# A two-layer attention and feed-forward kernel: values of every second key tile in column groups, V in columns of 17, K and Q weights with their columns in turns in one tile

## The chip, the cores and the metric

One core of one Trainium2 chip. The metric is the device time of one execution in microseconds, the median of a few runs. Engines named here: PE (TensorE, the matmul array), DVE (VectorE), ACT (ScalarE), POOL (GpSimd), SP (SyncE, which only issues transfers). SBUF is the working memory with 128 partitions, PSUM the memory that matmuls write to.

## The reference

`x` has 2048 rows of 512 values in bf16. The same two blocks are applied twice, with the same weights both times:

```python
def attention(x, wqkv, wo):            # 32 heads of 16 columns
    q, k, v = split(x @ wqkv)
    p = softmax(q @ k.T * 16 ** -0.5)  # 2048 x 2048 for each head
    return concat(p @ v) @ wo

x = x + attention(layernorm(x), wqkv, wo)
x = x + silu(layernorm(x) @ w1) @ w2   # w1 is 512 x 1792
x = x + attention(layernorm(x), wqkv, wo)
x = x + silu(layernorm(x) @ w1) @ w2
```

## The kernel before

**Tiles.** Rows are taken in 16 tiles of 128 (`TT`), and queries in 4 chunks `c` of 512 rows (`NQC`). The 32 heads are taken in 8 head groups `hb` of 4 (`HB`). A head has 16 columns, and each head sits in a strip of 32 partitions: in `KT` and `QT`, head `j` of a group is in partitions 32j to 32j+15, row 32j+16 holds a one (K) or a bound on the score with a minus sign (Q), and the rest is zero. So one matmul over 32 rows gives the scores minus their bound, and the exp needs no maximum. The zeros come from padded weights: `wk_pad` and `wq_pad` hold each head's 16 weight columns followed by 16 zeros. POOL clears both (L81, L82) and copies the columns in (L114, L118) from `wraw`, the transferred weights.

**The loop.** A *unit* is one key tile `kt` of one head group of one chunk: 4 x 8 x 16 = 512 units in a layer. In a unit, `emit_s` (L518) makes the scores of the *next* unit: 4 matmuls, one for each head, each on its own 32 rows, into two PSUM tiles of two banks (`wide`, 3 buffers). ACT makes two exps (L586), each of 128x1024, from PSUM into `p_sb` (5 buffers). Then `emit_pv` (L530) multiplies by the values, 4 matmuls into `o_ps` (one buffer of one bank, 128 partitions x 512): two of the second exp of the unit before and two of the first exp of this unit. In a unit with `kt` = 0 only the two of the unit before are issued, and unit 1 then has six.

**The values** for head `j` come from `vdq`: a 128x128 operand that is zero but for columns 32j to 32j+15, which hold V, and column 32j+16, which holds ones, so that row 32j+16 of `o_ps` is the sum of the exps. POOL fills these operands from V, for 4 key tiles at a time into one of two slots (`vd_fill`, L139; `NG` = 4, `NR` = 2), 4 copies each, one for each head.

**The end of a head group.** When a head group's last values are in, DVE copies `o_ps` to `oT` (L574), PE transposes it (L337), DVE divides by the sums (L343, L344). These stand first in the queue described next.

**The pump.** All other work is cut into small steps in a queue, `Pump` (L487); each unit runs `todo` of them after its value matmuls, one in most units, two where many are left. A step is mostly two matmuls of 512 columns. In chunk 0 the steps are the K projections of the next head group (`k_piece`, L234); in every chunk the Q projection of the next (`q_piece`, L294); in chunks 1 to 3 the output projection of the chunk before (L355), its feed-forward part (L411), and in layer 0 the next layer's normalisation and V (`next_pieces`, L450). The order on PE, ACT and DVE is the order in which the program writes it; POOL's is set by a scheduler.

**Start and ends.** At the start the four chunks are normalised: statistics on DVE (L150, L151), a root on ACT, `xn` on DVE (L183), transposes on PE (L195), a copy on DVE (L196). Then follow K for head group 0 (`k_two`, L250), the largest K values (`amax_bm`, L260), Q (L294) and, in layer 0, V (`v_two`, L288). Between the layers and at the end, the last chunk's projection and feed-forward part (`ffn_last`, L468) run by themselves.

Of the kernel before, what the change touches and what calls it, by code (L numbers as in the profile page):

```python
# [9 lines left out]
ALU = mybir.AluOpType  # L10
# [8 lines left out]
def kernel(  # L19
# [17 lines left out]
    H = 32  # L37
# [9 lines left out]
    VS = DH + 1  # L47
    KR = 32
    NG = 4
    NR = 2  # L50
# [6 lines left out]
    vpool = ctx.enter_context(tc.tile_pool(name="vpool", bufs=2))  # L57
    qpool = ctx.enter_context(tc.tile_pool(name="qpool", bufs=3))
# [6 lines left out]
    small = ctx.enter_context(tc.tile_pool(name="small", bufs=4))  # L65
# [13 lines left out]
    wq_pad = wpool.tile([P, CT, H, 32], BF16, name="wq_pad")  # L79
    wk_pad = wpool.tile([P, CT, H, 32], BF16, name="wk_pad")  # L80
    nc.gpsimd.memset(wk_pad[:], 0.0)  # L81
    nc.gpsimd.memset(wq_pad[:], 0.0)  # L82
    cw = cpool.tile([P, 256], BF16, name="cw")
    nc.vector.memset(cw[:], 0.0)
    nc.vector.memset(cw[0:1, 128:129], 1.0)
    for j in range(4):
        nc.vector.memset(cw[0:1, 32 * j + 16 : 32 * j + 17], 1.0)
# [6 lines left out]
    onescol = cpool.tile([P, 1], FP32, name="onescol")  # L94
    mc_ps = narrow("mc_ps")
    nc.tensor.matmul(mc_ps[:, 0:1], lhsT=cw[0:1, 0:128], rhs=cw[0:1, 128:129], start=True, stop=True)
    nc.vector.tensor_copy(out=onescol[:], in_=mc_ps[:, 0:1])


# [9 lines left out]
    w2_sb = wpool.tile([P, FT, D], BF16, name="w2_sb")  # L109
    wraw = htpool.tile([P, CT, 2 * D], BF16, name="wraw", tag="ht")  # L110
    nc.scalar.dma_start(wraw[:], A_wqkv[:, 0 : 2 * D].rearrange("(ct p) f -> p ct f", p=P))
    nc.scalar.dma_start(wv_sb[:], A_wqkv[:, 2 * D : 3 * D].rearrange("(ct p) f -> p ct f", p=P))
    for ct in range(CT):
        nc.gpsimd.tensor_copy(  # L114
            out=wk_pad[:, ct, :, 0:DH],
            in_=wraw[:, ct, D : 2 * D].rearrange("p (h d) -> p h d", d=DH),
        )
        nc.gpsimd.tensor_copy(  # L118
            out=wq_pad[:, ct, :, 0:DH],
            in_=wraw[:, ct, 0:D].rearrange("p (h d) -> p h d", d=DH),  # L120
        )
# [7 lines left out]
    vs = [vpool.tile([P, TT, D], BF16, name=f"v{i}", tag="v") for i in range(2)]  # L129
    vdq = []  # L130
    for i in range(NR):
        vd = xpool.tile([P, NG, 4, P], BF16, name=f"vd{i}")
        nc.gpsimd.memset(vd[:], 0.0)
        for j in range(4):
            nc.gpsimd.memset(vd[:, :, j, 32 * j + DH : 32 * j + DH + 1], 1.0)
        vdq.append(vd)


    def vd_fill(va, hb, g, slot):  # L139
        for j in range(4):  # L140
            h = 4 * hb + j
            nc.gpsimd.tensor_copy(  # L142
                out=vdq[slot][:, :, j, 32 * j : 32 * j + DH],
                in_=va[:, NG * g : NG * (g + 1), DH * h : DH * (h + 1)],
            )
# [78 lines left out]
    def k_mm(xnT, hb, ps, cts):  # L224
        for ct in cts:
            nc.tensor.matmul(  # L226
                ps,
                lhsT=wk_pad[:, ct, 4 * hb : 4 * hb + 4, :].rearrange("p h s -> p (h s)"),
                rhs=xnT[:, ct, :],
                start=(ct == 0),  # L230
                stop=(ct == CT - 1),
            )

    def k_piece(xnTs, c, hb):  # L234
        cell = {}

        def a():
            cell["ps"] = narrow("k_ps")
            k_mm(xnTs[c], hb, cell["ps"][:, :], (0, 1))

        def b():
            k_mm(xnTs[c], hb, cell["ps"][:, :], (2, 3))
            nc.vector.tensor_scalar(  # L243
                out=KT[:, hb, c * 512 : (c + 1) * 512], in0=cell["ps"][:, :],
                scalar1=onescol[:, 0:1], scalar2=None, op0=ALU.add,
            )

        return [a, b]

    def k_two(xnTs, c, hb):  # L250
        k_ps = wide("k2_ps")
        for i in range(2):
            k_mm(xnTs[c + i], hb, k_ps[:, i, :], range(CT))
        nc.vector.tensor_scalar(
            out=KT[:, hb, c * 512 : (c + 2) * 512],
            in0=k_ps[:].rearrange("p a b -> p (a b)"),
            scalar1=onescol[:, 0:1], scalar2=None, op0=ALU.add,
        )

    def amax_bm(hb):  # L260
        nc.vector.tensor_reduce(
            out=amax[:, hb : hb + 1], in_=KT[:, hb, :], axis=AX.X, op=ALU.max,
            apply_absolute_value=True,
        )
        nc.vector.tensor_scalar_mul(out=Bm[:, hb, :], in0=E[:, :], scalar1=amax[:, hb : hb + 1])
# [8 lines left out]

    def v_piece(cellx, tt, va):
        cell = {}

        def a():
            cell["ps"] = narrow("v_ps")
            v_mm(cellx["xnT"], tt, cell["ps"][:, :], (0, 1))  # L280

        def b():
            v_mm(cellx["xnT"], tt, cell["ps"][:, :], (2, 3))
            nc.vector.tensor_copy(out=va[:, tt, :], in_=cell["ps"][:, :])

        return [a, b]

    def v_two(xnT, tt, va):  # L288
        ps = wide("v2_ps")
        for i in range(2):  # L290
            v_mm(xnT, tt + i, ps[:, i, :], range(CT))
        nc.vector.tensor_copy(out=va[:, tt : tt + 2, :], in_=ps[:, :, :])

    def q_piece(xnTs, c, hb, QTs):  # L294
        cell = {}

        def mm(cts):
            for ct in cts:
                nc.tensor.matmul(  # L299
                    cell["ps"][:, :],  # L300
                    lhsT=wq_pad[:, ct, 4 * hb : 4 * hb + 4, :].rearrange("p h s -> p (h s)"),
                    rhs=xnTs[c][:, ct, :],
                    start=(ct == 0),
                    stop=(ct == CT - 1),
                )
# [5 lines left out]
        def b():  # L311
            mm((2, 3))
            qc = qwork.tile([P, 512], BF16, name="qc", tag="qc")
            nc.vector.tensor_copy(out=qc[:], in_=cell["ps"][:, :])  # L314
# [7 lines left out]
        def d():  # L322
            nc.tensor.matmul(  # L323
                cell["ps"][:, :], lhsT=Bm[:, hb, :], rhs=cell["qu"][:], start=False, stop=True,
                skip_group_check=True,
            )
            QTs[c][hb] = qpool.tile([P, 512], BF16, name="QT", tag="qt")
            nc.vector.tensor_copy(out=QTs[c][hb][:], in_=cell["ps"][:, :])  # L328
# [84 lines left out]
    def ffn_pieces(c, emit_out):  # L413
        cell = {}
        pieces = ln_steps(c, cell)
        for ft in range(FT):
# [11 lines left out]
            def d(ft=ft, hc=hc):  # L428
                t_sb = tpool.tile([P, 2, 512], FP32, name="t_sb", tag="t")
                nc.scalar.activation(t_sb[:, 0, :], hc["ps"][:, :], ACT.Tanh, scale=0.5)  # L430
                nc.vector.scalar_tensor_tensor(  # L431
                    out=cell["hT"][:, ft, :], in0=t_sb[:, 0, :], scalar=1.0, in1=hc["ps"][:, :],
# [35 lines left out]
    def ffn_last(c, emit_out):  # L468
# [3 lines left out]
        for f2 in range(FT // 2):  # L472
# [3 lines left out]
            t_sb = tpool.tile([P, 2, 512], FP32, name="t_sb", tag="t")  # L476
# [41 lines left out]
    def emit_s(QT, hb, kt):  # L518
        tiles = [wide("s_ps") for _ in range(2)]
        for j in range(4):  # L520
            nc.tensor.matmul(  # L521
                tiles[j // 2][:, j % 2, :],
# [5 lines left out]
        return tiles  # L528

    def emit_pv(o_ps, p_sb, kt, pr):  # L530
        for jj in range(2):
            j = 2 * pr + jj
            nc.tensor.matmul(  # L533
                o_ps[:, :],
                lhsT=vdq[kt // NG % NR][:, kt % NG, j, :],
                rhs=p_sb[:, jj, :],
                start=(kt == 0 and j == 0),
                stop=(kt == TT - 1 and j == 3),
            )

# [10 lines left out]
    for L in range(2):  # L551
# [17 lines left out]
        s_now = emit_s(QTs[0][0], 0, 0)  # L569
# [6 lines left out]

        for u, (c, hb, kt) in enumerate(units):
            if kt == 0:
                if hb == 0:
                    old_attn, attn_c = (attn, c - 1)  # L580
                    new_attn = apool.tile([P, 4, D], BF16, name="attn", tag="attn")

            ps = []
            for pr in range(2):
                p_sb = ppool.tile([P, 2, 512], BF16, name="p_sb", tag="p")
                nc.scalar.activation(  # L586
                    p_sb[:].rearrange("p a b -> p (a b)"),
                    s_now[pr][:].rearrange("p a b -> p (a b)"),
                    ACT.Exp,
                    scale=float(SCALE),  # L590
                )
                ps.append(p_sb)

            if u + 1 < len(units):
                nc_, nhb, nkt = units[u + 1]
                s_now = emit_s(QTs[nc_][nhb], nhb, nkt)

            if kt == 0:
                for args in pend:
                    emit_pv(*args)  # L600
                pend = []
# [10 lines left out]
                pend = [(o_ps, ps[0], 0, 0), (o_ps, ps[1], 0, 1)]  # L612
# [11 lines left out]
            else:  # L624
                pend.append((o_ps, ps[0], kt, 0))
                for args in pend:
                    emit_pv(*args)
                pend = [(o_ps, ps[1], kt, 1)]

            if kt % NG == 0 and u > 0 and u + NG * (NR - 1) < len(units):  # L630
                _, fhb, fkt = units[u + NG * (NR - 1)]
                vd_fill(va, fhb, fkt // NG, fkt // NG % NR)
# [5 lines left out]
            if left and kt < TT - 2 and pump.q:  # L638
                todo = max(todo, 1)
            pump_some(todo)  # L640
# [5 lines left out]
        for args in pend:  # L646
            emit_pv(*args)
# [37 lines left out]
```

## Time and profile before

| | us |
|---|---|
| median of 3 runs (2173.24 to 2178.0) | 2176.86 |
| the profiled execution's own time | 2173.48 |
| its span in the profile | 2171.7 |
| first exp of layer 0, first exp of layer 1 (start) | 64.4, 1146.6 |
| end of the last exp of layer 0, of layer 1 | 1058.0, 2111.8 |
| ACT busy, PE busy | 1942.9, 1934.3 |

Times in the profile count from the span's start. A group's line gives the source line, the engine, the operation, what it writes and reads, the count; then the busy time and the mean of one instruction in ns; then the idle time of the engine just before these instructions, and what ended it. Instructions on one engine overlap in the records, so the mean of one (1249 ns for an exp) is longer than the distance from one to the next (0.92 us). A line of waits gives the engine and what waited, for what, the sum in us, the count and the longest. A line of the windows view is a stretch of time: its length, the busy time and instruction count of each engine, then PE's granted clock (1.00 is full), the share of the DMA engines and GB/s.

### The profile page before, as it was taken

To read this page: it belongs to the slowest core of one execution; us is meant where nothing else is said; L and a number is where in the kernel's file an instruction comes from. 1 tells how busy PE (TensorE), PEld (TensorE's weight loads), DVE (VectorE), ACT (ScalarE), POOL (GpSimd) and SP (SyncE) were. 2 spreads that over 40 slices of the span, in tenths; PEclk is the share of its full clock that TensorE was granted. 3 is DMA by queue.
4 is the path that set the end of the run, shared out by engine and by line. 5 is a ranking of instruction groups with operands and counts; after the bars stand their busy time and mean duration, and the time that the engine had idled before them with its cause. 6 is when DMAs were issued, how large, how long until landed. Compare 5 with 4: busy or idle time off the path is not lost.

```text
span 2171.7 us, 28490 instructions
## 1 busy us (share of the span) xinstructions
PE 1934.3 (89%) x10355; PEld 712.9 (33%) x10561; DVE 558.7 (26%) x1106; ACT 1942.9 (89%) x2152; POOL 247.7 (11%) x1055
## 2 busy tenths in 40 slices
PE   3999988899898998999778999998999889998996
PEld 1333323333333333333232333333333333333332
DVE  6323222112311133112342322131113111131114
ACT  0899989999899998999418999999999999999981
POOL 3111111111011110111000111111111111111100
PEclk9999999999999999999789999999999999999997
DMA  4000000000000000000000000000000000000000
GB/s 145 1 1 1 1 1 1 1 1 1 1 1 1 1 1 1 1 1 1 1 0 1 1 1 1 1 1 1 3 8 1 1 1 8 4 1 1 6 5 10
DMA packets 8477, 11.79 MB, mean 5 GB/s; under 512 B 400, under 2 KB 7312, under 8 KB 8336
## 3 DMA queue, kind: packets, MB, share of 16 engines
q1 hardware_dynamic: 7280, 8.39, 1.1%
q8 instruction: 82, 1.34, 0.2%
q10 hardware_dynamic: 1056, 1.57, 0.2%
q14 instruction: 59, 0.48, 0.1%
HBM read 7.86 MB, written 2.10 MB: 5 GB/s over the span
## 4 chain that ended last, share of the span: by engine, by line
PE 62%; ACT 22%; issue 9%; DVE 6%; DMA 0%; ACTq 0%; DVEq 0%
PE o_ps L533 29%; ACT p_sb L586 20%; PE s_ps L521 16%; PE y_ps L400 3%; PE k_ps L226 3%; PE q_ps L299 2%; PE h_ps L393 2%; PE y_ps L372 2%; PE v_ps L270 2%; ACT t_sb L430 1%; DVE st L150 1%; PE t_ps L195 1%; DVE oT L574 1%; PE at_ps L337 1%; DVE hT L478 1%
## 5 line engine op out<-in xcount | busy, mean ns | idle before, releaser
L586 ACT ACTIVATE p_sb<-s_ps 128x1024 bf16<-128x1024 f32 x2048 | 1921.3, 1249 | 105.2 <-PE s_ps L521 105.2
L533 PE MATMUL o_ps<-p_sb,vd 128*128 128x512 bf16 x3909 | 1034.4, 383 | 19.6 <-issue 15.3
L521 PE MATMUL s_ps<-QT,KT 32*128 32x512 bf16 x4096 | 574.5, 383 | 89.9 <-ACT p_sb L586 85.7
L533 PEld LDWEIGHTS <-vd 128*128 128x128 bf16 x4096 | 317.7, 98 | 478.6 <-issue 237.4
L142 POOL COPY vd<-v 128x64 bf16<-128x64 bf16 x1024 | 231.1, 238 | 1850.8 <-PE o_ps L533 1708.8
L521 PEld LDWEIGHTS <-KT 32*128 32x128 bf16 x4096 | 175.2, 90 | 589.8 <-issue 569.1
L574 DVE CAST oT<-o_ps 128x512 bf16<-128x512 f32 x64 | 44.3, 692 | 381.1 <-PE o_ps L533 381.1
L431 DVE SCALAR_TENSOR_TENSOR hT<-t_sb,h_ps 128x512 bf16<-128x512 f32 x84 | 57.5, 685 | 301.7 <-ACT t_sb L430 301.7
L400 PE MATMUL y_ps<-w_sb,hT 128*128 128x512 bf16 x445 | 126.3, 383 | 5.4 <-DVE hT L478 4.5
L393 PE MATMUL h_ps<-xnT,w_sb 128*128 128x512 bf16 x438 | 127.0, 389 | 2.8 <-DVE xnT L196 1.0
L314 DVE CAST qc<-q_ps 128x512 bf16<-128x512 f32 x64 | 44.2, 691 | 170.3 <-PE q_ps L299 170.3
L243 DVE TENSOR_SCALAR KT<-k_ps,onescol 128x512 bf16<-128x512 f32 x56 | 42.0, 751 | 168.7 <-PE k_ps L226 168.7
L195 PE MATMUL t_ps<-ident,xn 128*128 128x128 bf16 x256 | 30.8, 263 | 57.2 <-DVE xn L183 55.4
L406 DVE SCALAR_TENSOR_TENSOR x_sb<-y_ps,x_sb 128x512 bf16<-128x512 f32 x32 | 22.1, 691 | 231.1 <-PE y_ps L400 231.1
L477 ACT ACTIVATE t_sb<-h_ps 128x1024 f32<-128x1024 f32 x14 | 14.3, 1023 | 74.9 <-PE h_ps L393 58.7
L430 ACT ACTIVATE t_sb<-h_ps 128x512 f32<-128x512 f32 x84 | 78.3, 932 | 0.0
L299 PE MATMUL q_ps<-xnT,wq_pad 128*128 128x512 bf16 x255 | 75.8, 380 | 2.5 <-DVE attn L344 2.4
L226 PE MATMUL k_ps<-xnT,wk_pad 128*128 128x512 bf16 x254 | 76.7, 392 | 0.3 <-issue 0.2
L393 PEld LDWEIGHTS <-w_sb 128*128 128x128 bf16 x448 | 44.8, 100 | 58.2 <-issue 8.6
L400 PEld LDWEIGHTS <-hT 128*128 128x128 bf16 x448 | 43.9, 99 | 60.1 <-DVE hT L478 5.6
L328 DVE CAST QT<-q_ps 128x512 bf16<-128x512 f32 x64 | 44.3, 692 | 36.6 <-PE q_ps L323 36.6
L372 PE MATMUL y_ps<-wo_sb,aT 128*128 128x512 bf16 x126 | 40.6, 423 | 7.6 <-DVE aT L367 7.3
(58 smaller groups left out, 568.2 us busy)
## 6 DMA issues: line engine op xcount, KB each, us to landing
w_sb<-in_B_w_dram SPq DMA_DIRECT2D x2, 1792.0 KB, 14.9
x_sb<-in_A_x_dram SPq DMA_DIRECT2D x4, 512.0 KB, 9.8
out_dram<-x_sb SPq DMA_DIRECT2D x16, 128.0 KB, 1.7
wraw<-in_A_wqkv_dram ACTq DMA_DIRECT2D x1, 1024.0 KB, 7.6
wv_sb<-in_A_wqkv_dram ACTq DMA_DIRECT2D x1, 512.0 KB, 10.0
wo_sb<-in_A_wo_dram SPq DMA_DIRECT2D x1, 512.0 KB, 12.4
```

The source lines that it names most:

```text
L142: nc.gpsimd.tensor_copy(out=vdq[slot][:, :, j, 32 * j : 32 * j + DH], in_=va[:, NG * g : NG * (g + 1), DH * h : DH * (h + 1)],)
L226: nc.tensor.matmul(ps, lhsT=wk_pad[:, ct, 4 * hb : 4 * hb + 4, :].rearrange("p h s -> p (h s)"), rhs=xnT[:, ct, :], start=(ct == 0), stop= ...
L299: nc.tensor.matmul(cell["ps"][:, :], lhsT=wq_pad[:, ct, 4 * hb : 4 * hb + 4, :].rearrange("p h s -> p (h s)"), rhs=xnTs[c][:, ct, :], star ...
L372: nc.tensor.matmul(cell["ps"][:, :], lhsT=cell["aT"][:, ct, :], rhs=wo_sb[:, ct, :], start=(ct == 0), stop=(ct == CT - 1),)
L393: nc.tensor.matmul(ps, lhsT=w1_sb[:, ct, ft * P : (ft + 1) * P], rhs=xfT[:, ct, :], start=(ct == 0), stop=(ct == CT - 1),)
L400: nc.tensor.matmul(ps, lhsT=hT[:, ft, tq * P : (tq + 1) * P], rhs=w2_sb[:, ft, :], start=(ft == 0), stop=(ft == FT - 1),)
L430: nc.scalar.activation(t_sb[:, 0, :], hc["ps"][:, :], ACT.Tanh, scale=0.5)
L431: nc.vector.scalar_tensor_tensor(out=cell["hT"][:, ft, :], in0=t_sb[:, 0, :], scalar=1.0, in1=hc["ps"][:, :], op0=ALU.add, op1=ALU.mult,)
L521: nc.tensor.matmul(tiles[j // 2][:, j % 2, :], lhsT=KT[32 * j : 32 * j + KR, hb, kt * P : (kt + 1) * P], rhs=QT[32 * j : 32 * j + KR, :], ...
L533: nc.tensor.matmul(o_ps[:, :], lhsT=vdq[kt // NG % NR][:, kt % NG, j, :], rhs=p_sb[:, jj, :], start=(kt == 0 and j == 0), stop=(kt == TT - ...
L574: nc.vector.tensor_copy(out=oT[:], in_=o_ps[:])
L586: nc.scalar.activation(p_sb[:].rearrange("p a b -> p (a b)"), s_now[pr][:].rearrange("p a b -> p (a b)"), ACT.Exp, scale=float(SCALE),)
```

## The change

- **Columns of 17.** V is kept as `va`, one for each layer: for each key tile 32 heads x 17 columns (16 of V and a one), and 15 columns more at the end. POOL sets both tiles to one at the start; V is copied into the 16 columns of each head. The two-tile V copy becomes two copies.
- **Column groups.** For odd key tiles (`COL`) the values are multiplied without `vdq`: for each head, a matmul whose stationary operand is 32 columns of `va` (the head's 17 and 15 that belong to the next) writes 32 partitions of `o_ps`. Both pairs of an odd tile are issued in the next unit. Even key tiles (`DIAG`) go as before, through `vdq`, which holds two of them a slot (`NG` = 2).
- **Weights.** `wkq` replaces `wk_pad` and `wq_pad`: 16 columns of K and 16 of Q in turns for each head. The K projection reads it from column 0 on, the Q projection from column 16. What the other operand leaves in the upper half of a strip is multiplied by zero when PSUM is copied out (`own` is one in the first 16 partitions of each strip). The Q bound is now a matmul of its own that DVE adds to `qc`.
- **Constants** (`own`, `onescol`, `one17`, `lead`) are made by DVE reductions of the identity instead of a small matmul.
- **Code that isn't used here.** `exp_passes`, `epool`'s `z`, `m` and `pd`, and `late` serve key tiles in `OFF`, which is empty: all exps stay on ACT.
- Pools: `qpool` 3 to 2 buffers, `small` 4 to 3; the second layer's `va` and the first's are separate tiles.

```diff
+    NG = 2
+    COL = [1, 3, 5, 7, 9, 11, 13, 15]
+    DIAG = [kt for kt in range(TT) if kt not in COL]
+    OFF = []
...
-    nc.gpsimd.memset(wk_pad[:], 0.0)
-    nc.gpsimd.memset(wq_pad[:], 0.0)
...
+    cols = cpool.tile([P, 4], FP32, name="cols")
+    idr = ident[:].rearrange("p (j r) -> p j r", r=32)
+    nc.vector.tensor_reduce(out=cols[:, 0:1], in_=idr[:, :, 0:DH], axis=AX.XY, op=ALU.max)
...
+    own, onescol, one17, lead = (cols[:, i : i + 1] for i in range(4))
...
+    wkq = wpool.tile([P, CT, 2 * D + DH], BF16, name="wkq")
+    nc.gpsimd.memset(wkq[:, :, 2 * D : 2 * D + DH], 0.0)
     for ct in range(CT):
+        pairs = wkq[:, ct, 0 : 2 * D].rearrange("p (h t d) -> p h t d", t=2, d=DH)
+        for t in range(2):
+            nc.gpsimd.tensor_copy(
+                out=pairs[:, :, t, :],
+                in_=wraw[:, ct, (1 - t) * D : (2 - t) * D].rearrange("p (h d) -> p h d", d=DH),
+            )
...
+    VW = VS * H + 32 - VS
+    for i in range(2):
+        va = xpool.tile([P, TT, VW], BF16, name=f"va{i}")
+        nc.gpsimd.memset(va[:], 1.0)
...
         vd = xpool.tile([P, NG, 4, P], BF16, name=f"vd{i}")
         nc.gpsimd.memset(vd[:], 0.0)
...
+                out=vdq[slot][:, :, j, 32 * j : 32 * j + VS],
+                in_=va[:, k0 : k0 + step * (NG - 1) + 1 : step, VS * h : VS * h + VS],
...
-            scalar1=onescol[:, 0:1], scalar2=None, op0=ALU.add,
+            scalar1=own, scalar2=onescol, op0=ALU.mult, op1=ALU.add,
...
-        nc.vector.tensor_copy(out=va[:, tt : tt + 2, :], in_=ps[:, :, :])
+        for i in range(2):
+            nc.vector.tensor_copy(
+                out=v_dst(va, tt + i), in_=ps[:, i, :].rearrange("p (h d) -> p h d", d=DH)
+            )
...
-            nc.vector.tensor_copy(out=qc[:], in_=cell["ps"][:, :])
+            nc.vector.tensor_scalar(
+                out=qc[:], in0=cell["ps"][:, :], scalar1=own, scalar2=one17,
+                op0=ALU.mult, op1=ALU.add,
+            )
...
-            nc.vector.tensor_copy(out=QTs[c][hb][:], in_=cell["ps"][:, :])
+            nc.vector.tensor_tensor(
+                out=QTs[c][hb][:], in0=cell["ps"][:, :], in1=cell["qc"][:], op=ALU.add
+            )
...
+    def emit_pv(o_ps, ps, hb, kt, prs, va):
+        for pr in prs:
+            for jj in range(2):
+                j = 2 * pr + jj
+                if kt in COL:
+                    h = 4 * hb + j
+                    nc.tensor.matmul(
+                        o_ps[32 * j : 32 * j + 32, :],
+                        lhsT=va[:, kt, VS * h : VS * h + 32],
+                        rhs=ps[pr][:, jj, :],
+                        start=False,
+                        stop=(kt == TT - 1),
+                        skip_group_check=True,
+                    )
+                else:
+                    d = DIAG.index(kt)
+                    nc.tensor.matmul(
+                        o_ps[:, :],
+                        lhsT=vdq[d // NG % NR][:, d % NG, j, :],
+                        rhs=ps[pr][:, jj, :],
+                        start=(kt == 0 and j == 0),
+                        stop=False,
+                        skip_group_check=True,
+                    )
...
+        def flush(u):
+            for args in pend:
+                emit_pv(*args, va)
+            pend.clear()
...
+                flush(u)
+                if off:
...
+                elif kt in COL:
+                    pend.append((o_ps, ps, hb, kt, (0, 1)))
+                else:
+                    emit_pv(o_ps, ps, hb, kt, (0,), va)
+                    pend.append((o_ps, ps, hb, kt, (1,)))
```

## The prediction

> **What bounds the kernel now.** I read the page's busy table first, then the groups, then the waits of ScalarE, then the stretches where ScalarE waits.
>
> ```profile
> span 2171.7 us, 28490 instructions
> PE 1934.3 (89%) x10355; PEld 712.9 (33%) x10561; DVE 558.7 (26%) x1106; ACT 1942.9 (89%) x2152; POOL 247.7 (11%) x1055
> L586 ACT ACTIVATE p_sb<-s_ps 128x1024 bf16<-128x1024 f32 x2048 | 1921.3, 1249 | 105.2 <-PE s_ps L521 105.2
> L533 PE MATMUL o_ps<-p_sb,vd 128*128 128x512 bf16 x3909 | 1034.4, 383 | 19.6 <-issue 15.3
> L521 PE MATMUL s_ps<-QT,KT 32*128 32x512 bf16 x4096 | 574.5, 383 | 89.9 <-ACT p_sb L586 85.7
> ...
> ACT p_sb L586 <- PE s_ps L521: 105.2, 54, 43.1
> ```
>
> PE and ACT show the same share, but the groups tell them apart. The exps fill 1921.3 us, 0.92 us each back to back, so a unit (one key tile, two exps) can't take under 1.84 us. Of the 105.2 us that exps waited for scores, 28.0 and 43.1 lie before the first exp of each layer. Only 34.1 us is left inside both attention loops: 28.4 in the first head group of chunks 1, 2 and 3 of layer 0 (9.4, 9.4 and 9.6 in the waits view), 2.0 at the start of layer 1, and the rest in pieces of 0.16 at key tile 3 of a head group. That 34.1, with some 0.1 per restart, is all that a faster PE can give back. The rest of the span is 64.4 us of start, 88.6 between the layers and 60 of tail.
>
> The second thing to see is the clock of PE and what goes before its changes (windows view: PE, PEld, DVE, ACT and POOL busy, then granted clock):
>
> ```profile
> 327.89:331.31 3.42, 1.36 (x6) 0.40 (x5) 2.93 (x16) 2.74 (x3) 0.00 (x0) 1.00 0.00 0
> 331.31:334.72 3.41, 2.97 (x15) 1.41 (x16) 1.12 (x4) 1.94 (x2) 0.43 (x2) 0.50 0.02 5
> 805.76:809.17 3.41, 2.08 (x12) 0.53 (x10) 1.01 (x3) 3.41 (x4) 0.90 (x4) 1.00 0.02 7
> 809.17:812.59 3.42, 2.64 (x9) 0.82 (x11) 0.36 (x1) 1.52 (x3) 0.00 (x0) 0.50 0.00 0
> 833.06:836.48 3.42, 2.07 (x10) 0.49 (x8) 3.01 (x14) 3.42 (x4) 0.00 (x0) 1.00 0.02 5
> 836.48:839.89 3.41, 2.48 (x22) 1.23 (x23) 2.36 (x9) 1.80 (x3) 0.45 (x2) 1.00 0.00 0
> ```
>
> The clock changes only on a grid of 3.41 us. I recounted the matmul records on that grid: a 512-column matmul is 0.213 us of array (their spacing is 0.216), a 128-column transpose a quarter of that, and a score matmul, which uses 32 of 128 rows, also a quarter. The stretches at full clock that were followed by half clock held at most 0.36 (0.27 at 327.9, 0.33 at 805.8, 0.36 at 2154.0); the emptiest that kept it held 0.375, 0.377 and 0.379 (560.0, 833.1, 1782.0). Counting scores as whole breaks the order (0.45 at 805.8 lost the clock, 0.39 at 2113.1 kept it); three eighths each also separates them (0.36 and 0.39). Of stretches at half clock, nine of 0.80 or more went back up; one of 0.81 and all of 0.63 and below stayed. The one at 805.8 is the passage between two head groups: PE waits for oT and for attn, and all it has is 4 scores, 3 value matmuls and 4 transposes.
>
> **The change part by part.**
>
> *Values.* Per pair of units PE now issues 8 full value matmuls (1.73 us). After: 4 full (0.86) and one group of four on 32 columns each. No row shows such a group. Bounds: 0.21 if four run at once, 0.87 plus a switch if they follow each other. The nearest row is the four score matmuls on 32 rows, 0.43 us from first start to the next value matmul, switch included; I take that, a saving of 0.44 us a pair. ScalarE's pace covers it in most units. It shows in two places:
> - The wait at key tile 3: there are 22 of about 0.16 idle and 0.1 restart, and unit 1 loses two of six value matmuls (0.43). All go: -5.9 (bounds 0 and -8).
> - The three first head groups of layer 0, where the pump runs two steps a unit. The waits behind them are mostly PE waiting for DVE (oT 0.79, attn 0.81, qu 1.11, aT 0.52), and these stay. Odd units lose 0.43 and even ones almost nothing: over units 1 to 12 some 2.5 each of the 10.4 (9.4 and ten restarts), -7.5 (bounds 0 and -15). Late next is the same DVE chain.
>
> *The clock.* What PE loses in matmuls it loses in occupancy. Around a head group's end (units 15 and 0, one grid stretch) there are six value matmuls now; after, two full ones and a group of four that I count as quarters: three fewer by array, 3 x 0.213 / 3.41 = 0.19 less. Such stretches stand at 0.38 to 0.52 now, so they come to 0.2 to 0.33, under the 0.36 that lost the clock. I recounted the whole trace with the odd tiles' value matmuls as quarters one unit later: between the layers' starts and ends, 38 stretches are at or under 0.36, in 36 separate events, where 3 are now; with scores at three eighths it is 13; with scores and groups at a half, none. Price of one event: chunk 3's first two waits (half clock) sum to 4.3 us, chunk 1's same two (full clock) to 3.0, so 1.3; at the start of layer 1 three stretches at half clock cost one wait of 2.0, 0.7 each. By work: a unit after with two pump matmuls is about 1.4 to 1.5 us of PE, 2.8 to 3.0 at half clock against 1.84 of exps, so 3.41 x (1 - 1.84/2.9) = 1.25. I take 1.2, and 30 new events, nearest to the quarter that the grid supports best: +36 (bounds 0, and 44 x 1.3 = +57; three times that if the clock stays down).
>
> [...]
>
> *The start.* Removed: two POOL memsets of 128x4096 (3.5 us each) ahead of the weight copies. Added behind the copies: two memsets of va, 128x8944 each; at 3515 ns per 4096 that is 7.7 us each, then two of vd at half their size (0.9 each). DVE's normalisation runs beside them:
>
> ```profile
> 12.46 0.74 DVE L183 TENSOR_SCALAR xn<-x_sb,mvb,rstd 128x512 bf16<-128x512 bf16 x1
> 13.45 2.11 DVE L183 TENSOR_SCALAR xn<-x_sb,mvb,rstd 128x512 bf16<-128x512 bf16 x1
> ...
> 13.61 3.69 POOL L133 MEMSET vd<- 128x2048 bf16 x2
> ```
>
> An xn takes 0.40 alone. Beside POOL's 1.8 us memset it took 2.11, and ended 0.15 after the first of the two did; statistics and PSUM copies weren't stretched. The copies wait for wraw (8.45) and end at about 13.1, so va's first memset runs 13.1 to 20.8. The last xn of chunk 0 is released at 20.9 instead of 15.6: +5.4. Chunk 1's first xn would then start near 25.9, and the second memset ends at 28.5: +2.6. The vd memsets add up to 0.9 and the four small DVE reductions 0.2. Less some slack: +8.7, all on the path, since K waits for chunk 3. Bounds: 0 if the memsets don't hold DVE, +13 if an earlier xn is caught and both memsets are met in a row.
>
> [...]
>
> *The rest, at nothing.* KT with two column operands instead of one (751 ns): it and qc may gain 60 ns, 64 times or fewer, behind exps; at a layer's start 0.2. QT as an add: 688 against 692 in the rows of that form. V copies as two of 0.69 instead of 1.23: beside 1.73 us of V matmuls. POOL's fills are as many and half as long. The ring of two QT is written one head group after its last reader. The last group of a layer flushes four grouped matmuls instead of two.
>
> Sum: 8.7 - 5.9 - 7.5 + 36 = +31 on 2173.5 of the profiled execution, 2205. The median of the runs is 3.4 above that execution: 2208.
>
> **The rivals.**
> - *The clock holds.* Grouped matmuls or scores count as more than a quarter, so the passages stay above the limit; for it speaks that a half each gives no event. Then 8.7 - 5.9 - 7.5 = -5: 2172, within the measurement's resolution or, if the memsets don't hold DVE, 2164. This ends on the other side. It decides if fewer than about five events occur (4 x 1.2 = 5).
> - *Few events.* Scores at three eighths: 13 less 3, times 1.2 = +12, in all +7: 2184.
> - *The clock stays down.* A half-clock stretch must hold about 0.8 to come back; near passages PE waits for DVE, and a second and third stretch could follow. 30 x 2.5 x 1.2 = +90: 2262. Against it: all three in the loops came back after one.
> - *The groups don't overlap.* Four in a row cost what they do now plus a switch of 0.1. The gains go (+13) and occupancy in quarters falls just the same: 2222.
>
> **How the numbers follow.** Chances: the forecast 0.45, few events 0.19, clock holds 0.18, stays down 0.10, no overlap 0.08. The range runs from 2168 (clock holds, a little less start) to 2262 (stays down at 2.5 stretches); some 0.05 lies under it and 0.07 above. 0.2% is 4.4 us, about what a measurement of this kernel can tell. Faster (under 2172.5): two thirds of "clock holds" and a little, 0.13. Same: the rest of it and the low end of few events, 0.10. Slower: 0.77.
>
> **What would show it.** In the changed profile: 0.50 in the granted clock of some 30 stretches inside the loops, each after a head group's end, with a new exp wait of about 1.2 us behind it; the waits of 0.16 at key tile 3 gone; a first exp at about 73 us instead of 64.4, with xn of 7 us beside va's memset; four grouped value matmuls starting within 0.2 us. Wrong if the clock row in the loops stays as it is, or if the grouped matmuls count as whole.

## The result, and the profile after

The changed kernel takes 2209.55 us (median of 4 runs, 2208.5 to 2213.6) against 2175.05 for the kernel before (4 runs, 2173.24 to 2178.0). The ratio is 1.0161, with a 95% interval of 1.0141 to 1.018. The profiled execution took 2208.69 us, with a span of 2206.9. The forecast was 2208, in a range of 2168 to 2262.

From the changed kernel's page, the span, the busy times, the row of the granted clock and the groups that answer to those shown of before:

```profile
span 2206.9 us, 28693 instructions
PE 1879.2 (85%) x10560; PEld 596.5 (27%) x10560; DVE 579.3 (26%) x1111; ACT 1946.1 (88%) x2152; POOL 245.8 (11%) x1048
PEclk9999989999999998999778999899999999999997
L686 ACT ACTIVATE p_sb<-s_ps 128x1024 bf16<-128x1024 f32 x2048 | 1919.3, 1305 | 129.4 <-PE s_ps L555 127.7
L555 PE MATMUL s_ps<-QT,KT 32*128 32x512 bf16 x4096 | 705.6, 394 | 186.8 <-ACT p_sb L686 181.9
L580 PE MATMUL o_ps<-p_sb,vd 128*128 128x512 bf16 x2048 | 644.8, 404 | 0.0
L570 PE MATMUL o_ps<-p_sb,va 128*32 128x512 bf16 x2048 | 211.7, 402 | 1.3 <-ACT p_sb L686 1.0
```

PE is less busy (1879.2 us against 1934.3) and ACT's exps are the same (1919.3 against 1921.3), yet exps wait 22 us longer for scores (127.7 against 105.2). The clock row is below 9 in seven slices, against three in the row of before:

```profile
PEclk9999999999999999999789999999999999999997
```

One passage between head groups shows how. The windows view (busy of PE, PEld, DVE, ACT, POOL, then the granted clock) and PE's timeline for the same stretch, then ACT's:

```profile
283.99:287.41 3.42, 2.07 (x16) 0.69 (x14) 0.69 (x1) 3.42 (x5) 0.43 (x2) 1.00 0.00 0
287.41:290.83 3.42, 3.42 (x17) 0.94 (x14) 0.68 (x2) 2.76 (x3) 0.00 (x0) 0.50 0.02 5
```

```profile
285.59 0.39 PE L555 MATMUL s_ps<-QT,KT 32*128 32x512 bf16 x2 [0.53 <-ACT p_sb L686]
285.91 0.40 PE L570 MATMUL o_ps<-p_sb,va 128*32 128x512 bf16 x4
287.14 0.40 PE L370 MATMUL at_ps<-ident,oT 128*128 128x128 bf16 x4 [0.83 <-DVE oT L661]
287.47 0.61 PE L555 MATMUL s_ps<-QT,KT 32*128 32x512 bf16 x4
288.02 1.89 PE L580 MATMUL o_ps<-p_sb,vd 128*128 128x512 bf16 x4
```

```profile
291.23 1.02 ACT L686 ACTIVATE p_sb<-s_ps 128x1024 bf16<-128x1024 f32 x1 [1.06 <-PE s_ps L555]
```

In the stretch to 287.41 PE has little: scores, two full value matmuls, one group of four and the transposes that begin at its end; none of its gaps shown there is over 0.83 us. The granted clock is 0.50 in the next 3.42 us, where unit 1's four full value matmuls take 1.89 us instead of about 1 (four took 1.04 at full clock in the kernel before); the exp behind them waits 1.06 us.

Where the span's +35.2 us comes from, with the first and last exps as marks:

| us | start | loop 0 | between | loop 1 | tail | half-clock events (stretches) in the loops |
|---|---|---|---|---|---|---|
| before | 64.4 | 993.6 | 88.6 | 965.3 | 59.8 | 3 (3) |
| after | 73.7 | 1006.3 | 90.8 | 976.6 | 59.5 | 39 (51) |
| difference | +9.3 | +12.7 | +2.2 | +11.3 | -0.3 | +36 (+48) |

An event is a fall of the granted clock to 0.50 inside a loop; it lasts one or more stretches of 3.41 us. The loops are counted from a layer's first exp to the end of its last; half-clock stretches that begin in the first 5 us of a loop are left out.

Of the 39 events 28 begin at a passage (key tiles 15, 0, 1 and 2); the other 11 lie at key tiles 7 and 11 to 13.

### The profile page after: what moved, and what is told of

Read it like the earlier page. It is cut to its first block, busy times and chain, and to the rows that moved or that the text cites. A ratio compares the mean times of both kernels' runs of the same rounds, so it can differ in the third digit from the quotient of the medians.

```text
span 2206.9 us, 28693 instructions
## 1 busy us (share of the span) xinstructions
PE 1879.2 (85%) x10560; PEld 596.5 (27%) x10560; DVE 579.3 (26%) x1111; ACT 1946.1 (88%) x2152; POOL 245.8 (11%) x1048
## 4 chain that ended last, share of the span: by engine, by line
PE 43%; ACT 35%; issue 15%; DVE 7%; DMA 0%; ACTq 0%; DVEq 0%
ACT p_sb L686 33%; PE s_ps L555 14%; PE o_ps L580 12%; PE o_ps L570 5%; PE k_ps L239 2%; PE h_ps L426 2%; PE y_ps L433 1%; PE y_ps L405 1%; PE q_ps L327 1%; ACT t_sb L463 1%; PE v_ps L290 1%; DVE st L163 1%; PE at_ps L370 1%; DVE oT L661 1%; PE t_ps L208 1%
## 5 line engine op out<-in xcount | busy, mean ns | idle before, releaser
L686 ACT ACTIVATE p_sb<-s_ps 128x1024 bf16<-128x1024 f32 x2048 | 1919.3, 1305 | 129.4 <-PE s_ps L555 127.7
L555 PE MATMUL s_ps<-QT,KT 32*128 32x512 bf16 x4096 | 705.6, 394 | 186.8 <-ACT p_sb L686 181.9
L580 PE MATMUL o_ps<-p_sb,vd 128*128 128x512 bf16 x2048 | 644.8, 404 | 0.0
L155 POOL COPY vd<-va 128x34 bf16<-128x34 bf16 x1024 | 222.5, 219 | 1880.3 <-PE o_ps L580 1839.0
L570 PE MATMUL o_ps<-p_sb,va 128*32 128x512 bf16 x2048 | 211.7, 402 | 1.3 <-ACT p_sb L686 1.0
L580 PEld LDWEIGHTS <-vd 128*128 128x128 bf16 x2048 | 125.3, 99 | 250.6 <-issue 240.1
L342 DVE TENSOR_SCALAR qc<-q_ps,cols 128x512 bf16<-128x512 f32 x64 | 51.8, 810 | 175.2 <-PE q_ps L327 175.2
L256 DVE TENSOR_SCALAR KT<-k_ps,cols 128x512 bf16<-128x512 f32 x56 | 45.4, 810 | 172.4 <-PE k_ps L239 172.4
L570 PEld LDWEIGHTS <-va 128*32 128x32 bf16 x2048 | 53.2, 93 | 125.0 <-issue 124.7
L327 PE MATMUL q_ps<-xnT,wkq 128*128 128x512 bf16 x256 | 81.0, 401 | 2.4 <-DVE attn L377 2.4
L239 PE MATMUL k_ps<-xnT,wkq 128*128 128x512 bf16 x256 | 80.6, 409 | 0.3
```

Of the source, the lines that this page charges most:

```text
L155: nc.gpsimd.tensor_copy(out=vdq[slot][:, :, j, 32 * j : 32 * j + VS], in_=va[:, k0 : k0 + step * (NG - 1) + 1 : step, VS * h : VS * h + VS],)
L239: nc.tensor.matmul(ps, lhsT=wkq[:, ct, P * hb : P * hb + P], rhs=xnT[:, ct, :], start=(ct == 0), stop=(ct == CT - 1),)
L327: nc.tensor.matmul(cell["ps"][:, :], lhsT=wkq[:, ct, P * hb + DH : P * hb + DH + P], rhs=xnTs[c][:, ct, :], start=(ct == 0), stop=(ct == C ...
L555: nc.tensor.matmul(s_ps[:, jj, :], lhsT=KT[32 * j : 32 * j + KR, hb, kt * P : (kt + 1) * P], rhs=QT[32 * j : 32 * j + KR, :], start=True, ...
L570: nc.tensor.matmul(o_ps[32 * j : 32 * j + 32, :], lhsT=va[:, kt, VS * h : VS * h + 32], rhs=ps[pr][:, jj, :], start=False, stop=(kt == TT ...
L580: nc.tensor.matmul(o_ps[:, :], lhsT=vdq[d // NG % NR][:, d % NG, j, :], rhs=ps[pr][:, jj, :], start=(kt == 0 and j == 0), stop=False, skip ...
```

## The experiments

Theory: a stretch of 3.41 us in which PE holds less than about 0.375 of the array's time, a score or grouped matmul counted by its share of the array, loses the clock for the next. The limit is an estimate from the trace of before, where the stretches that lost the clock were counted at 0.36 at most and the emptiest that kept it at 0.375. Rivals: the grouped matmuls themselves, or PE's waits for DVE at the passage, take the clock down; the exp waits have nothing to do with the clock; or it is the time in which PE is busy at all that counts. For the start: POOL's sets of `va` hold DVE, or the start is late for another reason.

### e1_pad_passage

```diff
+    PAD = [15, 0, 1]
...
         s_ps = wide("s_ps")
+        if pr == 0 and kt in PAD:
+            for jj in range(2):
+                nc.tensor.matmul(s_ps[:, jj, :], lhsT=ident[:, :], rhs=QT[:, :], start=True, stop=True)
```

> The changed kernel with two more full 128x128x512 matmuls ahead of the scores of key tiles 15, 0 and 1 of each head group (they write a score tile that the scores then overwrite), so that PE is fuller just where head groups end. Occupancy theory (a 3.41 us stretch that holds less than about 0.375 of the array's time loses the clock): each passage gains up to 0.25, half-clock events inside the loops fall from 38 to under 10, exp waits inside the loops from 53 us to 25 to 30, span 2207 to about 2185 (2178 to 2192). Rival, the grouped matmuls or PE's waits for DVE at the passage take the clock down whatever PE holds: about 38 events stay, span 2207 to 2215. Rival, the exp waits have nothing to do with the clock: waits stay at 53 us or grow.

Measured: 2172.0 us (10 runs, 2168.4 to 2178.2), ratio to before 0.999 (0.9978 to 1.0002). In the profiled run 6 events are left, three of them at key tile 11 or 12 of the first head groups of chunks 1 to 3 in layer 0; none is at a passage. The line of the core (span, clock) and ACT's waits:

```profile
core 0: 2166.7 us, clock 0.973
ACT p_sb L690 <- PE s_ps L559: 94.9, 26, 45.2
```

Same passage: the stretch in which PE waits for `oT`, the one behind it, and that wait in PE's timeline:

```profile
279.49:282.91 3.42, 2.59 (x21) 1.02 (x19) 1.37 (x3) 3.42 (x5) 0.00 (x0) 1.00 0.00 0
282.91:286.32 3.41, 3.25 (x22) 0.97 (x19) 1.10 (x2) 3.41 (x5) 0.72 (x4) 1.00 0.00 0
```

```profile
281.23 0.40 PE L371 MATMUL at_ps<-ident,oT 128*128 128x128 bf16 x4 [0.83 <-DVE oT L665]
```

PE was given more to do and the kernel became 40 us of span shorter. Inside the loops exps wait 21.6 us instead of 54.8, below what I had expected; loop 0 is 982.7 and loop 1 960.9, together 39.3 less than in the changed kernel, for 33 events fewer: 1.19 us each, net of what the added matmuls cost themselves. The expectation of the span (2178 to 2192) was too careful. The grouped matmuls and PE's waits for DVE are all still there (0.83 us for `oT` here, as in the changed kernel), so neither of them alone takes the clock down.

### e2_pad_middle

```diff
+    PAD = [6, 8, 10]
```

> The changed kernel with the same six matmuls a head group, ahead of the scores of key tiles 6, 8 and 10, away from the passages. Occupancy theory: the passages are as empty as before, 33 to 38 events, span 2203 to 2212. Rival, more work on PE anywhere keeps the clock up: as in the padded passage, about 2185.

Measured: 2214.9 us (4 runs, 2213.7 to 2216.4), ratio 1.0187 (1.0172 to 1.0203), 34 events in the profiled run. Its span of 2213.4 is 1.4 over what was expected.

```profile
core 0: 2213.4 us, clock 0.939
ACT p_sb L690 <- PE s_ps L559: 134.1, 66, 45.5
```

The same six matmuls in another place help nothing: the clock stays at 0.939 and exps wait 134.1 us, 39 more than with the matmuls at the passage. The loops (1012.7 and 977.0) are even 6.8 us longer than in the changed kernel, though with five events fewer, so matmuls added here cost time. Between these two runs the place decides and not the work in all (34 events here, 6 in e1), as the emptiest stretch would have it.

### e3_thin_values

The kernel before, with less value work instead of grouped value work. Three of four heads' values of odd key tiles are left out.

```diff
             j = 2 * pr + jj
+            if kt % 2 == 1 and j != 2:
+                continue
...
-                stop=(kt == TT - 1 and j == 3),
+                stop=(kt == TT - 1),
```

> The kernel before with one value matmul instead of four for each odd key tile (head 2 of the four; the other three heads' values of odd key tiles are left out), issued one unit later: the array's time of the change without column groups, without va and with the old start. Occupancy theory: passages as empty as in the changed kernel, 25 to 40 half-clock events in the loops, each with a wait of about an exp, span 2185 to 2200 with the first exp at 64.4. Rival, column groups themselves lower the clock: 3 events as before, and the freed PE time shows as gain: span 2155 to 2165.

Measured: 2200.8 us (4 runs, 2193.1 to 2204.3), ratio 1.0121 (1.0092 to 1.015), first exp at 64.4, 37 events, loops 1005.9 and 974.7, against 993.6 and 965.3 with all the values.

```profile
core 0: 2195.6 us, clock 0.941
276.80:280.21 3.41, 2.10 (x16) 0.69 (x15) 0.69 (x1) 3.41 (x5) 0.47 (x2) 1.00 0.00 0
280.21:283.63 3.42, 3.42 (x16) 0.94 (x14) 0.68 (x2) 2.69 (x3) 0.00 (x0) 0.50 0.00 0
```

This kernel has no column group, and loses the clock about as often as the changed one (37 events against 39). It leaves out three eighths of all value matmuls and is 1.2% slower. So column groups as such aren't needed for the fall.

### e8_pad_rows

As e1, with matmuls on 32 rows in place of the full ones:

```diff
-                nc.tensor.matmul(s_ps[:, jj, :], lhsT=ident[:, :], rhs=QT[:, :], start=True, stop=True)
+                nc.tensor.matmul(
+                    s_ps[:, 0, :], lhsT=KT[0:KR, hb, kt * P : (kt + 1) * P], rhs=QT[0:KR, :],
+                    start=True, stop=True,
+                )
```

> As the padded run, with the six added matmuls of a head group on 32 of 128 rows (a copy of the first head's scores, written to where the scores then go) instead of 128: the same time on PE, a quarter of the array. If the clock goes by the share of the array that is used: a passage gains up to 0.06 instead of 0.25, 20 to 36 events stay, span 2188 to 2207. Rival, the clock goes by the time in which PE is busy at all: as with full matmuls, about 6 events, span 2163 to 2172.

Measured: 2195.4 us (4 runs, 2186.7 to 2204.8), ratio 1.0094 (1.0066 to 1.0122). In the profiled run (2186.7 us) 24 events and a span of 2184.9, 3 us under what was expected; the median agrees. The profiled run is the fastest of the four; the others' clock was 0.950 to 0.957.

```profile
core 0: 2184.9 us, clock 0.962
284.08:287.50 3.42, 2.48 (x20) 0.88 (x20) 0.98 (x3) 3.42 (x5) 0.43 (x2) 1.00 0.00 0
287.50:290.91 3.41, 3.19 (x13) 0.84 (x13) 0.39 (x1) 2.41 (x4) 0.00 (x0) 0.50 0.00 0
```

The same number of added matmuls of the same length (384, of 379 ns here and 382 in e1), in the same places: 24 events against 6. On a quarter of the rows they did less for the clock than in full, which speaks for the share of the array and against busy time. The rows show it at one passage: here PE is busy for 2.48 us of the stretch and the clock falls, in e1 for 2.59 and it stays, and in the kernel before 2.07 was enough to keep it (833.06).

### e6_more_groups

```diff
-    COL = [1, 3, 5, 7, 9, 11, 13, 15]
+    COL = [1, 2, 3, 5, 6, 7, 9, 10, 11, 13, 14, 15]
```

> The changed kernel with 12 of 16 key tiles in column groups instead of 8. Occupancy theory: units without pump steps hold only about 0.23 + 0.1 of the array, so low stretches appear off the passages too: more than 70 stretches at half clock in the loops (51 in the changed kernel), mean clock under 0.93; each costs less since PE has less to do, span 2205 to 2235. Rival, PE time is what counts: PE has less work, exp waits shrink, span under 2200 with no more stretches at half clock.

Measured: 2228.2 us (4 runs, 2226.5 to 2231.8), ratio 1.0246 (1.0232 to 1.0261), 64 events of 109 stretches.

```profile
core 0: 2224.7 us, clock 0.895
PEclk9898879999888998899778898799998989989987
```

Less array time again, more half clock (109 stretches against 51), and a longer run. Half of the falls now come in the middle of head groups (32 of 64 at key tiles 3 to 13, against 11 of 39). The price of a stretch looks smaller: the loops grew by 19.7 us for 58 more stretches, though some of that may be what the lighter value matmuls gave back.

### e7_no_groups

```diff
-    NG = 2
+    NG = 4
...
-    COL = [1, 3, 5, 7, 9, 11, 13, 15]
+    COL = []
```

> The changed kernel with no column groups: all 16 key tiles through the padded operand, four key tiles a fill as before; V in columns of 17, the weights in turns and the constants stay. Theory: clock and loops of the kernel before (3 to 5 events, 993.6 and 965.3 within 3), the late start (73 to 74) and the 2 us between the layers stay: span 2180 to 2186. Rival, the columns of 17 or the weights in turns slow the loops by themselves: loops 5 us or more longer than before.

Measured: 2183.0 us (5 runs, 2181.9 to 2187.6), ratio 1.0041 (1.0026 to 1.0055). Loops 995.2 and 965.1, 4 events, first exp at 75.2.

```profile
core 0: 2183.0 us, clock 0.977
```

The columns of 17, the weights in turns and the new constants cost nothing that shows in the loops (1.6 us more in the first, with one event more, and none in the second). Their cost is the start, 10.8 us here (1.2 later than expected). The 2 us between the layers did not stay (88.8): over all runs that part lies between 87.4 and 90.9, so no cause is named for it.

### e4_small_set

```diff
-        nc.gpsimd.memset(va[:], 1.0)
+        ones = va[:, :, 0 : VS * H].rearrange("p t (h s) -> p t h s", s=VS)
+        nc.gpsimd.memset(ones[:, :, :, DH : DH + 1], 1.0)
+        nc.gpsimd.memset(va[:, :, VS * H : VW], 1.0)
```

> The changed kernel with the set of va cut to what isn't overwritten later: the column of ones of each head (16x32 elements) and the 15 spare columns, for each of the two tiles. Theory (POOL's two 7.7 us sets hold DVE's xn): first exp at 64 to 66 instead of 73.7, everything behind it 8 to 9.5 earlier, span 2197 to 2200 (the events may fall elsewhere by a few us). Rival, the start is late for another reason (DVE's reductions, the order of the copies): first exp stays at 72 to 74, span 2207.

Measured: 2200.8 us (4 runs, 2199.5 to 2202.9), ratio 1.0123 (1.0108 to 1.0138), first exp at 65.1, span 2200.1. In the changed kernel's timeline the two engines stood against each other like this (DVE, then POOL):

```profile
13.37 7.38 DVE L196 TENSOR_SCALAR xn<-x_sb,mvb,rstd 128x512 bf16<-128x512 bf16 x1
...
25.66 3.77 DVE L196 TENSOR_SCALAR xn<-x_sb,mvb,rstd 128x512 bf16<-128x512 bf16 x2
```

```profile
12.91 15.33 POOL L142 MEMSET va<- 128x8944 bf16 x2
28.19 2.12 POOL L147 MEMSET vd<- 128x1024 bf16 x2
```

An xn of 0.4 us took 7.38, until the first set was done, and one in the next chunk 2.73, until the second was. With short sets in the same place 8.6 of the 9.3 us are back, and the same xn takes 2.32:

```profile
13.26 2.32 DVE L198 TENSOR_SCALAR xn<-x_sb,mvb,rstd 128x512 bf16<-128x512 bf16 x1
```

The start's cost is the sets.

### e5_pad_and_set

The edits of e1 and e4 together.

> Both at once: the six full matmuls a head group around the passages, and the small set of va. Theory: the two are independent; first exp near 65, loops as in the padded run (982.7 + 960.9, within 4), span 2155 to 2163, time 2157 to 2167, a ratio of about 0.994 to the kernel before. Rival (the start's shift only moves the grid of stretches, and events come back elsewhere): more than 10 events, span 2167 or more.

Measured: 2167.3 us (5 runs, 2166.4 to 2168.8), ratio 0.9966 (0.9953 to 0.9978): a little faster than both kernels, but short of what was expected. First exp at 68.7, loops 988.0 and 960.2, 10 events.

```profile
13.35 4.75 DVE L199 TENSOR_SCALAR xn<-x_sb,mvb,rstd 128x512 bf16<-128x512 bf16 x1
```

```profile
12.90 2.42 POOL L144 MEMSET va<- 128x512 bf16 x1
14.92 0.61 POOL L145 MEMSET va<- 128x240 bf16 x1
15.47 2.27 POOL L144 MEMSET va<- 128x512 bf16 x1
17.34 0.61 POOL L145 MEMSET va<- 128x240 bf16 x1
```

Here one xn stood through all four sets; in e4 the xn of the same place took 2.32 us and got in between. The bad end of the range for the start, an xn that meets two sets in a row, does occur. Why there are 10 events and not 6 is not shown: the grid of stretches stands differently against the program in the traces (it begins 0.2 us behind the span's start in the kernel before, 0.7 in the changed one, 3.0 in e1), and the next run, with an earlier start still, has 6 again. So whether the two edits are independent stays open.

### e9_early_set

As e5, with the tiles and sets of `va` and `vd` written ahead of the weight copies:

```diff
     nc.gpsimd.memset(wkq[:, :, 2 * D : 2 * D + DH], 0.0)
+    VW = VS * H + 32 - VS
+    vs = []
+    for i in range(2):
+        va = xpool.tile([P, TT, VW], BF16, name=f"va{i}")
...
     for ct in range(CT):
```

> The run with both repairs (six full matmuls a head group around the passages, small sets of va), with POOL's sets of va and vd moved ahead of the weight copies, into the time in which POOL waits for the transferred weights. In the run with both, one xn still stood 4.75 us beside two sets of 2.3 us each. Theory (only POOL instructions that run at the same time hold DVE): xn at 0.4 to 0.75, first exp at 61 to 64.5 instead of 68.7, span 2156 to 2163, time 2158 to 2165, ratio 0.993 to 0.996. Rival (the sets fill POOL up to 9 us and push the weight copies, which then meet the xn of chunks 0 and 1): first exp at 65 or later, span 2163 or more.

Measured: 2161.4 us (6 runs, 2158.9 to 2169.8), ratio 0.9949 (0.9932 to 0.9965). First exp at 63.7, loops 982.8 and 961.0, 6 events. DVE's timeline at the same xn:

```profile
core 0: 2157.3 us, clock 0.973
12.14 0.74 DVE L197 TENSOR_SCALAR xn<-x_sb,mvb,rstd 128x512 bf16<-128x512 bf16 x1
13.13 0.40 DVE L197 TENSOR_SCALAR xn<-x_sb,mvb,rstd 128x512 bf16<-128x512 bf16 x1
```

The sets now run from 1.97 to 8.7 us, while POOL waits for the weights (for 6.3 us in the changed kernel), and the xn takes its 0.40 us. This is the fastest of the versions here.

## Why the prediction was right

- **The bound.** Right. Exps took 1919.3 us after, 1921.3 before; the freed PE time could only come back out of 34.1 us of waits.
- **The clock, +36 from 30 events at 1.2.** Right in kind, and shown by e1, e2 and e3; right in place for 28 of the 39 events. There are 36 events more, and e1 gives 1.19 us each. I had rounded the 36 of the recount with quarters down to 30. The limit of 0.375 holds up nearly: counted in the changed kernel with each matmul's array time from the start of its record, of 46 stretches that lost the clock all but three (0.377, 0.385, 0.399) hold under 0.375, and of 507 that kept it all but eight (0.31 to 0.37) hold that or more. With grouped matmuls as whole, the fullest stretch that lost it would hold 0.59, and 47 that kept it no more than that. That a quarter of the rows counts less than the whole is shown by e8; that it is exactly a quarter is only the best fit. The 0.213 us of a 512-column matmul is half of the 0.427 from one to the next at a granted clock of 0.50 (0.216 at full clock); a 128-column transpose follows another after 0.107 and 0.056.
- **The readings behind the clock.** The stretch at 560.0, put at 0.375, comes to 0.44 by the prediction's own weights (five full matmuls, four scores, four transposes), and the one at 805.8 to 0.31; counted so, those that lost the clock hold at most 0.36 and those that kept it at least 0.37, so the order stands. The trace of the kernel before has 10355 matmuls for 10561 weight loads, so some stretches held more than was counted, the half-clock one at 809.17 among them (9 for 11). So what a half-clock stretch needs to come back is less sure than 0.80: in the changed kernel's trace, where none is missing, some of about 0.71 came back.
- **The values, -5.9 and -7.5.** Right in size: with the clock mostly held (three events more than before), e1's loops are 15.3 shorter than before (13.4 predicted), of which the three first head groups give 9.1. Of the 22 waits of about 0.16 at key tile 3 the changed kernel has 2 left. The group is quicker than I took it: its four matmuls start within 0.01 us of each other (in 510 of 512 groups), and the next full matmul follows 0.33 to 0.34 us after the first, where I took 0.43 from scores that start in two pairs; four scores that start together are followed after 0.33 in the kernel before too. In the changed kernel itself the gain is there, but more than spent.
- **The start, +8.7.** Measured +9.3, by the xn and the set that were named (13.37 to 20.75, then 25.66 to 28.39).
- **At nothing.** KT and qc went from 751 and 691 ns to 810, QT stayed at 692, and the V copies of the start take 688 each; e7's loops show that none of it is felt.
- **The sum.** 8.7 + 22.6 in the loops = 31 predicted; 9.3 + 24.0, 2.2 between the layers and -0.3 of tail = 35.2 measured. The 2.2 was not foreseen. The events were six too few (7 us), and at e1's price the gain was some 5 too small (36 x 1.19 - 24.0 = 18.8 for 13.4), which offset each other in part. The median came closer still, 2209.55 for 2208, because it lies 0.9 above the profiled execution and not the 3.4 taken over from before. The closeness of the number is partly luck.
- **The rivals.** "The clock holds" is what e1 made by hand, though with six matmuls more: its span is 5.0 under that of before (2171.7 to 2166.7), the -5 given for it. That its median is also the 2172 given is partly chance, since the kernel before took 2173.4 in the runs beside it. "Few events" and "stays down" did not happen: most events last one stretch (51 stretches in 39 events). "The groups don't overlap" fell with the 0.01 us.

## What to carry to other kernels

A cheaper matmul on an engine that isn't the bound can cost time: here PE was busy for 55 us less and the run took 1.6% longer, 24 of its 35 us inside the loops. Before work is taken off PE, count what its emptiest 3.4 us stretch will still hold (about 0.375 of the array's time parted most stretches of this kernel that kept the clock from those that lost it), matmuls on part of the array by about that part (24 events with 32 of 128 rows in e8, 6 with all in e1). Where a passage falls short, a few matmuls whose result is overwritten can be worth their time (40 us of span in e1), and here only there (e2's loops grew by 6.8). Long sets on POOL belong where DVE has no instruction like xn to run (one took 7.38 us beside a set of 7.69, and 0.40 with the sets moved ahead in e9; PSUM copies of 0.41 and statistics of 0.66 beside the set kept their times), or should be cut to what isn't written later (8.6 of 9.3 us came back in e4).

## What the runs showed that I had not expected

- Adding matmuls to PE shortened the span by 40 us (2206.9 to 2166.7), and leaving out three eighths of the value matmuls lengthened it by 24 (2171.7 to 2195.6).
- A POOL set of 512 elements in steps of 17 takes 2.3 us, while 8944 in a row take 7.69: the short set is 17 times smaller and only 3.4 times shorter.
- e1's ten runs spread from 2168.4 to 2178.2, with the mean clock between 0.967 and 0.973. Where the grid of stretches falls on the loop may be the reason; no second trace of e1 shows it.
